# A sequence mixer and FFN kernel: another order of the first loads, later loads in parts, and a new instruction order

## The chip, the cores and the metric

The kernel runs on one core of a Trainium2 chip. The metric is the device time of one execution in microseconds (us), as the median of runs, and lower is better. Profiles come from one execution each; "span" is the time from its first to its last instruction.

## The reference

Input and output are 2048 positions by 640 channels in bfloat16. What is computed:

```python
def A(q, k, v, shift_k, ssm_k, ssm_D):
    k_shift = sum(pad3(k)[t:t + S] * shift_k[:, 3 - t] for t in range(4))   # four taps
    kv = k_shift * v
    y = causal_convolution(kv, ssm_k) + kv * ssm_D      # over S = 2048, in the reference by FFT
    return q * y

def B(x, w_gate, w_up, w_down):                         # 640 -> 1728 -> 640
    return (silu(x @ w_gate) * (x @ w_up)) @ w_down

h   = A_q + A(layernorm(A_q), A_k, A_v, ...)
out = h + B(layernorm(h), ...)
```

The condensed lines above leave out batch, padding and the FFT calls.

## The kernel before, in words

**Blocks.** The 2048 positions are four blocks j = 0 to 3 of 512, and the 640 channels two halves c = 0, 1 of 320. A block sits on 128 partitions with four neighbouring positions each (b = 0 to 3), so that a k tile holds seven rows of 640 per partition: four own ones and three of halo for the taps.

**Per block and half.** kv_block makes kv: four multiplications with taps (kvm), additions (kva) and the product with v (kvv). In blocks 0 and 1 VectorE adds; in blocks 2 and 3 POOL issues accumulating transfers instead (kvd, line 1006), three per half, one after the other. The filter ssm_k is loaded and turned, in blocks 0 and 1 by TensorE (ktr, line 738, then the copies kte), in blocks 2 and 3 by a transposing load. Block 0 is transformed with dense tables den (dfK, dfX; the inverse is di). Blocks 1 to 3 use a two-stage transform: stage one (s1K, s1X), a shuffle between partitions by transfers on SP (shK, shX), stage two (s2K, s2X), products on VectorE (m1, m2, ac, cr, ci, all through line 831), the inverse (i2, shuffles rs, i1). All matmuls but the transposes have line 625, all PSUM evictions line 608 or 611 on ACT, 609 on VectorE.

**LayerNorm and FFN.** The first LayerNorm takes its sums on ACT (lines 960, 967), the second from bn_stats on VectorE (921). Both take the reciprocal root on POOL (nr, line 937: nr0j for the first norm of block j, nr1j for the second), then VectorE's nm (939), the normalized tiles hn (ACT 947 or VectorE 946), their transposes on TensorE (tr, line 1132) and evictions te. The FFN of a block has 13 pairs of five 512-wide matmuls (gu) and a last one for both, silu on ACT (line 1160), the product gm on VectorE, and eight columns of 14 or 15 matmuls for the down projection (dn). The FFN of one block fills TensorE while the next is mixed.

**What sets the order.** Every operation is recorded with its reads and writes. The list _ORDER gives each a rank, _WHO forces some evictions to ACT or VectorE, and a planner (schedule, with durations and a model of transfers, dma_model) deals the operations out in rank order to the engines as their inputs and buffers become free. Each engine then runs its list in that fixed order. Transfers go through the queues of SP, ACT and POOL, each in its order; weight pieces on POOL (wg, wu, gul, wd) wait for the piece before the last, and the first for x of block 1. The tile KIN that takes the k of a block has one buffer, so kin2 waits for block 1's last read of it.

Names of loads: taps (the four tap rows), kraw (a filter half; 256 KB and 64 KB pieces), kin, vin, x (a block of k, v, q), den00 to den13 (eight pieces of 256 KB of the dense tables), tab (the other tables), drow (ssm_D). In block 0 the k rows are the cells "m" and "s" of tile KIN0, "z" its zeroed first rows; all tap multiplications wait for all three.

Of the kernel before, what the change touches and what calls it, by code (L numbers as in the profile page):

```python
# [10 lines left out]
ALU = mybir.AluOpType  # L11
# [5 lines left out]
295 0 2 15 16 249 250 1 3 4 6 5 7 8 9 11 12 13 14 18 17 19 20 21 22 23 25 24 26 27 28 29 30 31 32 254 255 258 259 666 262 263 266 267 270 271 274 275  # L17
278 279 282 286 290 291 294 298 299 287 302 303 283 305 306 641 642 645 646 649 650 653 654 658 661 662 665 657 670 673 337 674 677 678 682 251 685
686 690 692 693 1093 1089 1090 1094 1097 1098 1101 1102 1105 1106 1109 1110 1113 1114 1117 1118 1121 1122 1125 1126 1129 1130 1133 1134 1137 1138 1140
1141 1489 1490 1493 1494 1497 1498 1501 1502 1505 1506 49 1509 1510 1513 1514 1517 1518 1521 1522 1525 1526 1529 1530 1533 1534 238 1537 1538 1540  # L20
1541 310 314 315 319 1176 323 324 328 332 333 341 342 697 701 702 706 710 711 719 720 724 728 729 1145 1149 1150 1154 1158 1159 1163 1167 1168 1172
1177 1545 1549 1550 1554 922 1558 715 1559 1563 1567 1568 1572 1576 1577 236 237 239 240 241 242 243 244 245 246 247 248 34 35 36 33 37 38 39 40 41 10
42 43 44 45 46 48 50 51 52 53 54 55 56 73 892 74 75 76 82 83 84 85 91 92 93 94 100 101 102 103 57 58 59 60 61 62 63 64 65 66 67 68 69 70 71 72 99 77
78 79 80 81 86 87 88 89 90 95 96 97 98 104 105 106 107 108 109 110 111 112 113 114 115 116 117 118 119 120 121 122 123 124 125 126 127 128 129 130 131
132 133 134 1429 151 152 153 154 160 161 162 163 169 170 171 172 178 179 180 181 135 136 137 138 139 140 141 142 143 144 145 146 147 148 149 150 155
156 157 158 159 164 165 166 167 168 173 174 175 176 177 182 183 185 186 187 188 189 190 191 192 193 194 195 196 197 198 199 200 201 202 203 204 205
206 207 184 208 209 1255 210 211 212 213 214 215 216 217 218 219 220 221 222 223 224 225 226 227 228 229 355 356 357 358 359 360 361 362 383 384 385
386 387 388 389 390 391 392 47 393 394 395 396 397 398 230 231 232 399 400 401 402 363 364 365 417 366 367 368 369 370 371 372 373 374 375 376 1561
377 378 379 380 381 382 403 404 405 406 407 431 408 432 409 410 411 412 413 414 415 416 418 419 420 421 422 423 424 425 426 427 428 429 430 435 436
437 438 439 440 441 442 451 443 444 445 446 447 448 449 450 452 453 454 455 456 457 458 459 460 461 462 463 464 433 434 465 466 467 468 469 470 471  # L30
472 473 474 475 476 477 478 479 480 481 482 483 484 485 486 487 488 490 491 492 513 514 515 516 517 518 519 520 521 522 523 524 525 526 527 528 233
234 235 529 530 531 532 493 494 496 497 498 499 500 502 503 504 505 506 507 508 509 533 510 534 511 535 512 536 537 538 539 540 541 542 543 544 545
546 308 547 548 549 551 552 554 555 556 557 558 559 560 561 562 565 550 566 567 568 553 569 570 571 572 573 574 575 576 577 578 579 580 581 582 583
584 771 585 586 587 588 589 590 591 592 593 594 563 564 595 596 597 598 599 600 601 602 603 495 604 605 606 607 608 609 610 611 612 613 614 343 344
345 346 347 348 349 350 351 352 353 354 615 616 617 793 618 620 621 622 623 624 619 625 626 627 628 629 630 632 633 634 635 636 631 637 638 730 731
732 733 734 735 736 737 738 739 740 741 742 755 756 757 758 759 760 761 762 783 784 785 787 788 789 790 791 792 794 795 796 797 798 799 800 801 802
763 764 765 766 767 768 769 770 772 773 779 774 780 775 781 776 782 777 803 778 804 805 806 807 808 809 810 811 812 1346 813 814 815 816 817 818 819
820 821 822 823 824 825 826 827 828 830 831 832 833 834 835 836 839 829 840 841 842 843 844 845 846 847 848 849 850 851 852 853 854 855 856 857 858
859 860 861 862 863 864 865 866 867 868 869 870 871 872 874 873 875 876 877 878 879 880 883 884 885 886 887 888 889 890 837 838 881 882 891 893 894
895 896 897 898 899 900 901 902 903 904 905 906 907 908 909 910 911 912 913 914 915 916 937 938 939 940 941 681 942 943 944 945 946 947 948 949 950  # L40
951 952 953 954 955 956 917 918 919 920 921 923 924 925 926 927 928 929 930 931 932 933 934 935 936 957 958 959 960 961 962 963 964 965 966 967 968
969 970 971 972 973 974 975 976 977 979 980 981 982 983 984 985 986 987 988 989 786 990 993 994 995 996 997 998 999 1000 1001 1002 1003 1004 1005 1006
1007 1008 1010 1011 1012 1147 1013 1014 1015 1016 1009 1017 1018 1019 1020 1021 1022 1023 1024 1025 1026 1027 1028 1029 1030 1031 1032 1033 978 1034
1037 689 1038 1039 1040 1041 1042 1043 1044 991 992 1035 1036 1045 1046 1047 1048 1049 1050 1051 1052 1053 1054 1055 1056 1057 1058 1059 1060 1061
1062 743 744 745 746 747 748 749 750 751 752 753 754 1063 1064 1065 1066 1067 1068 1069 1204 1070 1071 1072 1180 1073 1181 1074 1182 1075 1183 1076
1184 1077 1078 1079 1080 1081 1082 1083 1084 1085 1086 1178 1179 1185 1186 1187 1188 1189 1190 1203 1205 1206 1207 1208 1209 1210 1231 1232 1233 1234
1235 1236 1237 1238 1239 1240 1241 1242 1243 1244 1245 1246 1247 1248 1249 1250 1211 1212 1213 1214 1215 1216 1217 1218 1219 1220 1221 1222 1223 1224
1225 1226 1227 1228 1229 1230 1251 1252 1253 1254 1256 1257 1258 1259 1260 1261 1262 1263 1264 1265 1266 1267 1268 1269 1270 1271 1272 1273 1274 1275
1276 1277 1278 1279 1280 1283 1284 1285 1286 1288 1289 1290 1291 1292 1287 1293 1294 1295 1296 1297 1298 1299 1300 1301 1302 1303 1304 1305 1306 1307
1308 1309 1310 1311 1312 1281 1282 1313 1314 1315 1316 1317 1318 1319 1320 1321 1322 1323 1324 1325 1326 1336 1327 1328 1329 1330 1331 1332 1333 1334  # L50
1335 1337 1338 1339 1340 1361 1362 1363 1364 1366 501 1367 1368 1369 1370 1371 1372 1373 1374 1375 1376 489 1377 1378 1379 1380 1341 1342 1343 1344
1345 1347 1348 1349 1350 1351 1352 1353 1354 1355 1356 1357 1358 1359 1360 1381 1382 1383 1384 1385 1386 1387 1388 1389 1390 1391 1392 1393 1394 1395
1396 1397 1398 1399 669 1401 1402 1403 1404 1405 1406 1407 1408 1409 1410 1413 1414 1415 1416 1417 1418 1419 1420 1421 1422 1423 1365 1424 1425 1426
1427 1428 1440 1431 1432 1433 1434 1435 1436 1437 1438 1430 1439 1441 1444 1442 1411 1412 1443 1445 1446 1447 1448 1449 1450 1451 1452 1453 1454 1455
1456 1457 1458 1459 1460 676 1461 1462 1191 1192 1193 1194 1195 1196 1197 1198 1199 1200 1201 1202 1463 1464 1465 1466 1467 1468 1469 1470 1471 1472
1473 1474 1475 1476 1477 1478 1479 1480 1481 1482 1483 1484 1485 1486 252 253 256 257 260 261 264 265 268 269 272 273 276 277 280 281 284 285 288 289
292 293 296 297 300 301 304 307 309 311 312 313 316 317 318 320 321 322 325 326 327 329 330 331 334 335 336 338 339 340 639 640 643 644 647 648 651
652 655 726 656 659 660 663 664 667 668 671 672 675 679 680 683 684 687 1491 688 691 694 695 696 698 699 700 703 704 705 707 708 709 712 713 714 716
717 718 721 722 723 725 727 1087 1088 1091 1092 1095 1096 1099 1100 1103 1104 1107 1108 1111 1115 1116 1119 1400 1120 1123 1124 1127 1112 1128 1131
1132 1135 1136 1139 1142 1143 1144 1146 1148 1151 1152 1153 1155 1156 1157 1160 1161 1162 1164 1165 1166 1169 1170 1171 1173 1174 1175 1487 1488 1492  # L60
1495 1496 1499 1500 1503 1504 1507 1508 1511 1512 1515 1516 1519 1520 1523 1524 1527 1528 1531 1532 1535 1536 1539 1542 1543 1544 1546 1547 1548 1551
1552 1553 1555 1556 1557 1560 1562 1564 1565 1566 1569 1570 1571 1573 1574 1575
"""
_WHO = (
    "......................................................................................................................................................"
# [38 lines left out]
class Prog:  # L104
# [18 lines left out]
    def op(self, engs, fns, reads=(), writes=(), prio=0, reserve=(), after=(), dma=None, name=""):  # L123
        o = Op()
# [345 lines left out]
def bass_sequential_preLN__ssm_conv_h3__swiglu_ffn__prompt_kernel(  # L470
# [6 lines left out]
    R = 4  # L477
# [836 lines left out]
```

## Time and profile before

| | |
|---|---|
| median of 3 runs | 319.65 us (317.93 to 324.96) |
| the profiled execution | 320.28 us, span 318.5 us |
| busy: TensorE, VectorE, ACT, POOL | 289.2, 236.6, 195.7, 42.1 us |
| bytes moved, mean rate | 41.94 MB, 132 GB/s |
| granted TensorE clock, mean | 0.989 |
| first dense matmul; first gate matmul; first matmul of the last FFN | 17.44; 62.16; 271.12 us |

In timelines a line gives start, duration, engine, source line, operation, output <- input, shapes, count, and in brackets the idle time before it and what ended it. SPq, ACTq and POOL DMA lines are issues of transfers, not the transfers. L-numbers are lines of the kernel before; in the new file the same functions stand 5 to 12 lines further down.

### The profile page before, as it was taken

Reading aid. Unit: us, or ns where it says so; the run is one execution under the profiler, and the core shown is the slowest. Engines: PE = TensorE matmul, PEld = TensorE weight load, DVE = VectorE, ACT = ScalarE, POOL = GpSimd, SP = SyncE. Lnnn points to the kernel's source line nnn. Section 1 sums busy time; section 2 is a strip of 40 time slices with the busy share of each in tenths; the row PEclk is TensorE's granted clock in tenths of the full one; section 3 lists DMA queues with packets and bytes.
Section 4 is the critical chain, followed back from the end, with each engine's and each line's share of the span. In section 5 each row is a group of like instructions: output and inputs, shape, how many; then the busy total and the mean of one; then the engine's idle time right before and its main releaser. Section 6 shows DMA issues by size and latency. Waiting matters only on the chain.

```text
span 318.5 us, 5166 instructions
## 1 busy us (share of the span) xinstructions
PE 289.2 (91%) x1844; PEld 154.9 (49%) x1844; DVE 236.6 (74%) x456; ACT 195.7 (61%) x469; POOL 42.1 (13%) x52
## 2 busy tenths in 40 slices
PE   3399998789959999979999999988999999999996
PEld 0165764334424356645433475543444566444574
DVE  1869999559677999897899999998287847223331
ACT  4269898997955864946874857598985314222200
POOL 0020432530111014100112000421100001000000
PEclk9999999699999999999999999999999999999999
DMA  7999585865673659734914301545310120000011
GB/s 184 348 414 238 167 260 190 293 225 171 142 196 75 176 136 171 221 137 105 284 21 65 126 21 64 145 126 144 84 62 21 43 82 23 21 0 2 0 41 43
DMA packets 29789, 41.94 MB, mean 132 GB/s; under 512 B 7954, under 2 KB 24627, under 8 KB 29253
## 3 DMA queue, kind: packets, MB, share of 16 engines
q1 hardware_dynamic: 23106, 25.43, 24.8%
q0 software_dynamic: 5808, 15.48, 19.6%
q10 hardware_dynamic: 850, 0.69, 0.8%
q8 instruction: 15, 0.25, 0.3%
q14 instruction: 10, 0.08, 0.1%
HBM read 20.63 MB, written 2.62 MB: 73 GB/s over the span
## 4 chain that ended last, share of the span: by engine, by line
PE 55%; DVE 17%; ACT 10%; DMA 10%; SPq 3%; issue 2%; ACTq 1%; POOL 0%; DVEq 0%
PE ps L625 53%; DVE sb L831 15%; DMA sb<-sb 6%; ACT sb L608 5%; DMA sb<-in_A_ssm_k_dram 4%; SPq L616 3%; ACT sb L947 2%; DVE stt L921 1%; ACT sb L611 1%; ACT sb L1160 1%; PE ps L738 1%; ACTq L616 1%; PE ps L1132 1%; ACT sb L967 1%; DVE sb L1091 0%
## 5 line engine op out<-in xcount | busy, mean ns | idle before, releaser
L625 PE MATMUL ps<-sb 128*128 128x320 bf16 (+2 forms) x1204 | 222.9, 339 | 6.7 <-ACT sb L608 3.4
L831 DVE TENSOR_TENSOR sb<-sb 128x1280 bf16<-128x1280 bf16 (+2 forms) x244 | 157.7, 698 | 19.2 <-ACT sb L608 6.9
L625 PEld LDWEIGHTS ps<-sb 128*128 128x128 bf16 (+2 forms) x1204 | 114.6, 98 | 97.0 <-issue 6.8
L608 ACT ACTIVATE sb<-ps 128x320 bf16<-128x320 f32 (+1 forms) x264 | 103.4, 489 | 38.7 <-PE ps L625 26.7
L831 DVE TENSOR_TENSOR sb<-ps,sb 128x512 bf16<-128x512 f32 (+1 forms) x96 | 56.5, 602 | 51.3 <-PE ps L625 50.7
L625 PE MATMUL ps<-sb,tab 128*64 128x320 bf16 (+2 forms) x512 | 66.7, 306 | 11.5 <-DMA sb<-sb 5.5
L1160 ACT ACTIVATE sb<-ps 128x512 bf16<-128x512 f32 (+1 forms) x56 | 33.8, 603 | 42.1 <-PE ps L625 42.0
L625 PEld LDWEIGHTS ps<-sb,tab 128*64 128x64 f16 (+2 forms) x512 | 31.1, 101 | 49.6 <-issue 15.1
L947 ACT ACTIVATE sb<-sb,stt 128x320 bf16<-128x320 bf16 (+1 forms) x35 | 24.3, 727 | 10.7 <-DVE stt L939 10.7
L1006 POOL DMA_DIRECT2D sb<-sb x12 | 12.3, 1023 | 94.9 <-DVE sb L831 77.5
L611 ACT ACTIVATE sb<-ps 128x320 bf16<-128x320 f32 x48 | 17.4, 452 | 8.0 <-PE ps L625 7.9
L937 POOL TENSOR_TENSOR stt<-stt 128x2 f32<-128x2 f32 (+1 forms) x12 | 12.5, 1042 | 67.4 <-DVE stt L936 67.4
L921 DVE BATCH_NORM_STATS2 stt<-sb 128x6 f32<-128x320 bf16 x32 | 13.9, 472 | 0.0
L967 ACT ACTIVATE sb<-sb,stt 128x640 bf16<-128x640 bf16 x16 | 13.4, 839 | 0.6 <-DVE stt L963 0.5
L738 PE MATMUL ps<-sb 128*128 128x128 bf16 (+1 forms) x48 | 7.3, 254 | 6.4 <-DMA sb<-in_A_ssm_k_dram 6.4
L960 ACT ACTIVATE sb<-sb 128x640 bf16<-128x640 bf16 x16 | 11.9, 741 | 0.8 <-DMA sb<-in_A_q_dram 0.7
L738 PEld LDWEIGHTS ps<-sb 128*128 128x128 bf16 (+1 forms) x48 | 4.2, 117 | 10.3 <-DMA sb<-in_A_ssm_k_dram 7.1
L1132 PE MATMUL ps<-sb 128*128 128x128 bf16 x80 | 7.0, 241 | 2.0 <-ACT sb L608 1.9
L1132 PEld LDWEIGHTS ps<-sb 128*128 128x128 bf16 x80 | 5.6, 107 | 3.6 <-DVE sb L831 1.1
L946 DVE TENSOR_SCALAR sb<-sb,stt 128x640 bf16<-128x640 bf16 (+1 forms) x13 | 5.8, 451 | 1.1 <-PE ps L1132 0.8
L936 DVE TENSOR_SCALAR stt<-stt 128x2 f32<-128x2 f32 (+1 forms) x12 | 1.9, 160 | 4.8 <-ACT sb L967 4.8
L616 POOL DMA_DIRECT2D sb<-in_B_w_down_dram x6 | 4.3, 722 | 7.4 <-DMA sb<-in_B_w_down_dram 6.9
(26 smaller groups left out, 37.5 us busy)
## 6 DMA issues: line engine op xcount, KB each, us to landing
sb<-sb SPq DMA_DIRECT2D x72, 160.0 KB, 2.6
sb<-sb POOLq DMA_DIRECT2D x12, 320.0 KB, 4.3
out_dram<-sb SPq DMA_DIRECT2D x16, 160.0 KB, 1.8
sb<-in_A_k_dram POOLq DMA_DIRECT2D x2, 1120.0 KB, 7.9
sb<-cst_den SPq DMA_DIRECT2D x8, 256.0 KB, 11.6
sb<-in_B_w_down_dram POOLq DMA_DIRECT2D x3, 480.0 KB, 5.4
sb<-in_A_v_dram SPq DMA_DIRECT2D x2, 640.0 KB, 12.5
sb<-in_A_q_dram SPq DMA_DIRECT2D x2, 640.0 KB, 12.7
```

Source lines behind the costliest of these rows:

```text
L608: fns = {"act": lambda a: a.activation(out=dst(), in_=src(), func=ACTF.Copy), "dve": lambda v: v.tensor_copy(out=dst(), in_=src())}
L611: fns = {"act": lambda a: a.activation(out=dst(), in_=src(), func=ACTF.Copy, scale=scale), "dve": lambda v: v.tensor_scalar(out=dst(), in0 ...
L616: fns = [(lambda g, d=d, s=s: g.dma_start(d(), s())) for d, s in subs]
L625: return lambda t: t.matmul(o(), l(), r(), start=st, stop=sp)
L738: return t.transpose(B16(pt, b // 2, (b % 2) * CW + d * 128, pr), src, V(IDN, 0, pr, 0, pr))
L831: return lambda v: v.tensor_tensor(out=o(), in0=a(), in1=b_(), op=op)
L921: vec(dve1(CW, False), lambda v: v.bn_stats(st6(l, j, b, c), V(xt, b * D + c * CW, CW)), [(xt, (b, c))], [(ST, ("s", l, j, b, c))], prio, ...
L937: P.op({"pool": 1.05}, lambda g: g.tensor_tensor(out=y, in0=va, in1=stt[:, 420:420 + hi - lo], op=ALU.pow), c1 + [(ST, "half")], c3, prio, ...
L947: "act": lambda a: a.activation(out=dst(), in_=src(), func=ACTF.Identity, scale=rs(l, j, b), bias=tmv(l, j, 3)[:, b:b + 1])},
L967: P.op({"act": act_c(D) + 0.3}, lambda a, b=b, jt=jt: a.activation(out=V(jt, 0, D), in_=V(xt, b * D, D), func=ACTF.Square, bias=tmv(l, j, ...
L1132: fns = [lambda t, k=k, d=d, pk=pk: t.transpose(B16(pk, 0, d * 128, 128), V(hn[k], d * 128, 128), V(IDN, 0, 128)) for d in range(5)]
L1160: P.op({"act": act_c(n)}, lambda a: a.activation(out=dst(), in_=src(), func=ACTF.Silu), rd, wr, -1000, name=f"si{nm}", after=after)
```

## The change

1. *First loads.* Filter half 0 of block 0 (kraw00) goes to the head of SP's queue, then the four own k rows of all 128 partitions in one transfer ("m"), then the three halo rows of partitions 1 to 127 in two ("h"). The first tap multiplication waits for "m" alone. v and filter half 1 follow the first four den pieces, x follows the last but one; drow goes to ACT, which issues no filter or k load any more.
2. *Parts.* The k loads of blocks 2 and 3 are issued as four transfers of 32 partitions, v and x as two of 64, and each accumulating transfer as two of 64 partitions. Blocks 0 and 1 keep whole loads.
3. *The planner.* Other numbers in its model (shuffle issue, shuffle and transpose spacing, half clock at the start and in the filter turns), and new lists _ORDER and _WHO (not shown, 1578 ranks). They change no instruction but its place and, for some evictions, its engine.

The diff from the loads on, without the lists and the planner's clock:

```diff
@@ -658,9 +663,13 @@
         def load_kv(j, prio):
             kt = kins[j] = P.tile(f"kin{j}", "KIN")
             vt = vins[j] = P.tile(f"vin{j}", "VIN")
-            dma([(lambda: V(kt, 0, 7 * D), lambda: dram(K2, (B * j - 3) * D, [[R * D, 128], [1, 7 * D]]))], 1147, [], [(kt, c) for c in range(2)], prio,
+            def rows(t, src, o, n, k):
+                w = 128 // k
+                return [(lambda p=p: V(t, 0, n, p, p + w), lambda p=p: dram(src, o + R * D * p, [[R * D, w], [1, n]])) for p in range(0, 128, w)]
+
+            dma(rows(kt, K2, (B * j - 3) * D, 7 * D, 4 if j > 1 else 1), 1147, [], [(kt, c) for c in range(2)], prio,
                 name=f"kin{j}", eng="pool" if j > 1 else "sp")
-            dma([(lambda: V(vt, 0, 4 * D), lambda: dram(V2d, B * j * D, [[R * D, 128], [1, 4 * D]]))], 655, [], [(vt, c) for c in range(2)], prio + 1,
+            dma(rows(vt, V2d, B * j * D, 4 * D, 2 if j > 1 else 1), 655, [], [(vt, c) for c in range(2)], prio + 1,
                 name=f"vin{j}", eng="pool" if j > 1 else "sp")
 
         def kraw_rows(t, j, c, prio, eng):
@@ -685,7 +694,8 @@
 
         def load_x(j, prio):
             t = xts[j] = P.tile(f"x{j}", "XH")
-            o = dma([(lambda: V(t, 0, 4 * D), lambda: dram(X2, B * j * D, [[R * D, 128], [1, R * D]]))], 655, [],
+            ps_ = ((0, 64), (64, 128)) if j > 1 else ((0, 128),)
+            o = dma([(lambda a=a, b=b: V(t, 0, 4 * D, a, b), lambda a=a, b=b: dram(X2, (B * j + R * a) * D, [[R * D, b - a], [1, R * D]])) for a, b in ps_], 655, [],
                     [(t, (b, c)) for b in range(4) for c in range(2)], prio, name=f"x{j}", eng="pool" if j > 1 else "sp")
             if j == 1:
                 front["x1"] = [o]
@@ -699,16 +709,13 @@
             for c in range(2):
                 kraws[0, c] = P.tile(f"kraw0{c}", "TK")
 
-            def kin(p0, p1, o=0):
-                return (lambda: V(KIN0, o * D, (7 - o) * D, p0, p1), lambda: dram(K2, (R * p0 - 3 + o) * D, [[R * D, p1 - p0], [1, (7 - o) * D]]))
-
-            dma([kin(16, 128), kin(1, 16)], 1140, [], [(KIN0, "m")], -2001, name="kin0")
-            dma([kin(0, 1, 3)], 10, [], [(KIN0, "s")], -2003, eng="act", name="kin0z")
-            kraw_rows(kraws[0, 0], 0, 0, -2000, "act")
-            kraw_rows(kraws[0, 1], 0, 1, -1990, "act")
-            front["v0"] = [dma([(lambda: V(VIN0, 0, 4 * D), lambda: dram(V2d, 0, [[R * D, 128], [1, R * D]]))], 655, [], [(VIN0, c) for c in range(2)], -1990,
-                               name="v0")]
-            dma([(lambda: V(DROW, 0, D, 0, 1), lambda: dram(A_ssm_D, 0, [[D, 1], [1, D]]))], 1, [], [(DROW, 0)], -1980, name="drow")
+            def kin(p0, p1, lo, hi):
+                return (lambda: V(KIN0, lo * D, (hi - lo) * D, p0, p1), lambda: dram(K2, (R * p0 - 3 + lo) * D, [[R * D, p1 - p0], [1, (hi - lo) * D]]))
+
+            kraw_rows(kraws[0, 0], 0, 0, -2010, "sp")
+            dma([kin(0, 128, 3, 7)], 655, [], [(KIN0, "m")], -2001, name="kin0")
+            dma([kin(16, 128, 0, 3), kin(1, 16, 0, 3)], 490, [], [(KIN0, "h")], -2000, name="kin0h")
+            dma([(lambda: V(DROW, 0, D, 0, 1), lambda: dram(A_ssm_D, 0, [[D, 1], [1, D]]))], 1, [], [(DROW, 0)], -1980, eng="act", name="drow")
 
             def den_piece(h, iv, prio):
                 o = (iv * 4 + h) * 1024
@@ -716,9 +723,12 @@
 
             for h in range(R):
                 den_piece(h, 0, -1970 + h)
-            load_x(0, -1960)
+            front["v0"] = [dma([(lambda: V(VIN0, 0, 4 * D), lambda: dram(V2d, 0, [[R * D, 128], [1, R * D]]))], 655, [], [(VIN0, c) for c in range(2)], -1966,
+                               name="v0")]
+            kraw_rows(kraws[0, 1], 0, 1, -1965, "sp")
             for h in range(R):
-                last = den_piece(h, 1, -1950 + h)
+                last = den_piece(h, 1, -1960 + h)
+            load_x(0, -1950)
             front["den"] = [last]
             dma([(lambda: tab[:, :], lambda: tab_dram.ap())], 700, [], [(TAB, 0), (TAB, 1)], -1930, name="tab")
 
@@ -739,6 +749,7 @@
 
                     fns.append(f)
             turned[j, c] = pe(fns, 128, 37, [(kr, 0), (IDN, 0)], tc(pt), prio, reserve=[(kt, 0), (kt, 1)], name=f"ktr{j}{c}")
+            turned[j, c].slow = True
             for k in range(2):
                 evac(lambda k=k: V(kt, k * 2 * CW, 2 * CW), lambda k=k: B16(pt, k, 0, 2 * CW), 2 * CW, [(pt[k], 0)], [(kt, 0)] if k == 0 else [(kt, 1)], prio, fast=True,
                      name=f"kte{j}{c}")
@@ -988,22 +999,22 @@
             t0 = P.tile("t0", "TMP")
             t1 = P.tile("t1", "TMP")
 
-            def v4(t):
-                return V2(t, 0, CW, 4, CW)
-
-            def kw(o):
-                return V2(kt, o * D + c * CW, D, 4, CW)
+            def v4(t, a=None):
+                return V2(t, 0, CW, 4, CW, *((a, a + 64) if a is not None else ()))
+
+            def kw(o, a=None):
+                return V2(kt, o * D + c * CW, D, 4, CW, *((a, a + 64) if a is not None else ()))
 
             def mul(dst, jj):
                 vec(dve2(W4), tt(lambda: v4(dst), lambda: kw(3 - jj), lambda: tapb(jj), ALU.mult),
-                    ([(kt, c)] if j else [(kt, x) for x in "msz"]) + [(TAPS, (jj, c))], [(dst, 0)], prio, name=f"kvm{j}{c}")
+                    ([(kt, c)] if j else [(kt, x) for x in ("mhz" if jj else "m")]) + [(TAPS, (jj, c))], [(dst, 0)], prio, name=f"kvm{j}{c}")
 
             def add():
                 vec(dve2(W4), tt(lambda: V(t0, 0, W4), lambda: V(t0, 0, W4), lambda: V(t1, 0, W4), ALU.add),
                     [(t0, 0), (t1, 0)], [(t0, 0)], prio, name=f"kva{j}{c}")
 
             def acc(src, cells):
-                P.op({"pool": 1.0}, [lambda g: g.dma_start(v4(t0), src(), accum_op=ALU.add)],
+                P.op({"pool": 2.0}, [lambda g, a=a: g.dma_start(v4(t0, a), src(a), accum_op=ALU.add) for a in (0, 64)],
                      [(t0, 0)] + cells, [(t0, 0)], prio, dma=(656, "acc"), name=f"kvd{j}{c}")
 
             mul(t0, 0)
@@ -1015,12 +1026,12 @@
                 mul(t1, 3)
                 add()
             else:
-                acc(lambda: v4(t1), [(t1, 0)])
+                acc(lambda a: v4(t1, a), [(t1, 0)])
                 mul(t1, 2)
                 vec(dve2(W4), tt(lambda: kw(0), lambda: kw(0), lambda: tapb(3), ALU.mult),
                     [(kt, c), (TAPS, (3, c))], [(kt, c)], prio, name=f"kvm{j}{c}")
-                acc(lambda: kw(0), [(kt, c)])
-                acc(lambda: v4(t1), [(t1, 0)])
+                acc(lambda a: kw(0, a), [(kt, c)])
+                acc(lambda a: v4(t1, a), [(t1, 0)])
             hv = lambda: V2(vt, c * CW, D, 4, CW)
             kv_last[j, c] = vec(dve2(W4), tt(hv, hv, lambda: v4(t0), ALU.mult), [(t0, 0), (vt, c)], [(vt, c)], prio, name=f"kvv{j}{c}")
 
@@ -1259,13 +1270,14 @@
             kb, kind = o.dma
             if kind == "shuffle":
                 s = max(issued, dmafree[0])
-                dmafree[0] = s + 0.3
+                dmafree[0] = s + 0.45
                 return s + 1.65 + (1.6 if link[0] > issued else 0.0)
             if kind == "store":
                 return issued + 1.3
             if kind == "turn":
                 s = max(issued, link[0] + 1.0 if link[0] > issued + 2.0 else 0.0, turn[0])
-                turn[0] = s + 4.9
+                turn[0] = s + 3.4
+                dmafree[0] = max(dmafree[0], s + 2.4)
                 return turn[0]
             s = max(issued + (1.3 if o.eng == "pool" else 0.9), link[0])
             link[0] = s + kb / 322.0
```

What it makes of the queues, by name (a star gives the transfers of one operation):

```
SP before:   taps kin0*2 v0 drow den00 den02 den01 den03 x0 den10 den11 den12 den13 tab kin1 vin1 kraw10*2 kraw11*2 x1 ...
SP after:    taps kraw00*2 kin0 kin0h*2 den00 den01 den02 den03 v0 kraw01*2 den10 den11 den12 x0 tab den13 kraw11*2 kin1 vin1 kraw10*2 x1 ...
ACT before:  ident kin0z kraw00*2 kraw01*2 (then work)
ACT after:   ident drow (then work)
POOL before: dadd dadd nr00 wg0 wu0 wg1 wu1 wg2 wu2 gul nr10 nr10 gul wd kin2 wd wd nr01 wd wd wdl kvd20 vin2 kvd20 kvd20 kvd21 ...
POOL after:  dadd dadd nr00 wg0 wu0 wg1 wu1 wg2 wu2 kin2*4 gul gul nr10 nr10 wd wd kvd20*2 wd wd wd wdl vin2*2 nr01 kvd20*2 kvd20*2 ...
```

The heads of the other lists, to block 0's first transposes (TensorE) and second normalized tiles (VectorE), with runs of one kind shortened:

```
TensorE before: ktr00 ktr01 dfK0h0 dfX0 (h0-h3) dfK0 (h1-h3) di0h0 di0h1 dfX1, di0h2, di0h3 dfK1 ktr10 di1 with s1K10, s1X10 ktr11 s2X10 (5 of 8) tr00
TensorE after:  ktr00 dfK0 (h0, h1, half of h2) dfX0 dfK0 (rest) di0h0 di0h1 ktr01 di0h2 di0h3 dfX1 dfK1 ktr10 di1 with s1X10, s1K10 ktr11 s2X10 (8) s2K10 (1) tr00
VectorE before: kvm00 kvm00 kva00 ... kvv00 kvm01 kvm01 kva01 m1000 ... kvv10 ... nm10 kvm11 ... hn01 nm10 kvm11 kva11 hn03 kvv11
VectorE after:  kvm00 kte00 kvm00 kva00 ... kvv00 kvm01 kvm01 kva01 kvm01 m1000 ... kvv10 ... kva11 l1m0 va10 kvv11 nm10 hn01 nm10 kte11 hn03
end, before:    ... dn230 dn231 (10 of 14) tr30 tr30 dn231 (4) tr31 tr31 gu31
end, after:     ... dn230 (10 of 14) tr30 tr30 dn230 (4) tr31 tr31 dn231 (14) gu30
```

## The prediction

> **What bounds the kernel now.** I read the page first (busy shares, the chain), then the timeline of the first 30 us, the stretches of 10 us, the waits of TensorE, and the timeline of single engines where the chain changes hands.
>
> ```profile
> span 318.5 us, 5166 instructions
> PE 289.2 (91%) x1844; PEld 154.9 (49%) x1844; DVE 236.6 (74%) x456; ACT 195.7 (61%) x469; POOL 42.1 (13%) x52
> ...
> PE 55%; DVE 17%; ACT 10%; DMA 10%; SPq 3%; issue 2%; ACTq 1%; POOL 0%; DVEq 0%
> ```
>
> TensorE is the bound, but not in every stage: 45% of the chain is not its own. The losses are in two places. The first is the front:
>
> ```profile
> 9.14 9.64 DVE L831 TENSOR_TENSOR sb<-sb 128x1280 bf16<-128x1280 bf16 x11 [6.56 <-DMA sb<-in_A_k_dram]
> ...
> 12.58 2.09 PE L738 MATMUL ps<-sb 128*128 128x128 bf16 x12 [5.65 <-DMA sb<-in_A_ssm_k_dram]
> ...
> 17.44 8.47 PE L625 MATMUL ps<-sb 128*128 128x320 bf16 x52
> 21.50 4.55 DVE L831 TENSOR_TENSOR sb<-sb 128x640 bf16<-128x640 bf16 x8 [2.72 <-ACT sb L608]
> ```
>
> The dense transforms of block 0 start at 17.44, behind the filter turns. VectorE waits for k until 9.14, again until 21.50, and then hardly at all up to 59.5: its work, not TensorE's, sets when block 0 reaches its second LayerNorm.
>
> ```profile
> 50.00:60.00 10.00, 6.90 (x50) 3.64 (x49) 9.96 (x28) 9.74 (x23) 5.30 (x7) 0.87 0.59 175
> 60.00:70.00 10.00, 8.73 (x49) 3.47 (x48) 3.11 (x6) 9.94 (x24) 4.01 (x5) 0.78 0.76 286
> ```
>
> Columns: stretch, its length, busy PE, PEld, DVE, ACT, POOL, granted clock, DMA share, GB/s. TensorE is idle 4.4 us between 50 and 70, and part of that stretch runs at a lower clock (0.87, 0.78; in stretches of 2 us it is 0.50 from 58 to 64). From 70 on these holes, in TensorE's own timeline, are nearly all that is left, the second place:
>
> ```profile
> 89.95 1.52 PE L625 MATMUL ps<-sb,tab 128*128 128x320 bf16 x10 [1.15 <-DMA sb<-sb]
> 95.62 0.33 PE L625 MATMUL ps<-sb,tab 128*64 128x320 bf16 x2 [2.40 <-DMA sb<-sb]
> 140.75 1.10 PE L625 MATMUL ps<-sb,tab 128*128 128x320 bf16 x6 [1.88 <-ACT sb L608]
> 215.98 1.02 PE L625 MATMUL ps<-sb,tab 128*64 128x320 bf16 x8 [0.92 <-DMA sb<-sb]
> 271.12 44.52 PE L625 MATMUL ps<-sb 128*128 128x512 bf16 x247 [1.11 <-ACT sb L608]
> ```
>
> **The change, part by part.** The profiled execution took 320.28 us (span 318.5, 1.8 around it), 0.6 above the median 319.65. The sum is made against 320.28.
>
> *The ring's order.* Before, SP issues k (980 KB, then 15 rows) first and ACT the filter; 980 KB land 5.9 us after issue at 1.16, at 7.1, and the 15-row piece with the halo lets VectorE go only at 9.14. After, SP issues filter 00 (320 KB) and the 128 k rows (640 KB): 960 KB, so again about 7.1 for the first multiply, which now needs these alone. The halo is 488 KB more; at the 216 and 373 GB/s of the first two stretches that is 1.3 to 2.3 us, so 8.4 to 9.4; I take 8.5. Filter 00 should land near 4.5 to 5; its turn (2.09 us) ends near 7, and its copy, now second on VectorE (0.48), fits before the halo. ACT no longer issues six load pieces, so it starts its tap evictions (from 5.71) some 2.7 us earlier.
>
> VectorE then: seven operations of 0.83 from 8.5 end kv of column half 0 at 14.3 (15.9 before). Four operations of half 1 follow to 17.6. The first X transform of h0 is eight matmuls after 14.3, at most 2.1 us at half rate, and two evictions of 0.45: 17.3. So the 2.72 us wait shrinks to nothing, and the products start at 17.6, not 21.5, with one multiply and one copy more behind them (1.3): a lead of 5.2 us. TensorE keeps up: its 20 K matmuls stand before X and run from about 9, when the first dense table has landed (1.7 MB by then). The second filter half and v come later in the ring, at some 13 and 14 us, but its turn stands behind the first inverse transforms, past 20.
>
> *What the lead is worth.* From the products to the second hn tile of block 0 the new VectorE order has the three filter copies in place of two K evictions and one copy (no difference), one normalization less (0.37) and the last kv multiply of block 1 ahead (0.82): 4.75 us left. That multiply and two more stand ahead of the first normalization too, so ACT's hn00 and the first LayerNorm transpose (57.42) come 2.9 us sooner; but TensorE has four spectrum groups more behind it (0.7): 3.6 us. What is late next is POOL: rstd of block 0 (54.32) now stands behind four kin2 issues and both gul pieces, which wait for the up and gate weights.
>
> ```profile
> 46.06 0.87 POOL L616 DMA_DIRECT2D sb<-in_B_w_up_dram  x1 [1.61 <-DMA sb<-in_B_w_up_dram]
> 54.32 2.21 POOL L937 TENSOR_TENSOR stt<-stt 128x2 f32<-128x2 f32 x2 [2.81 <-DVE stt L936]
> ```
>
> The last weight piece landed 6.4 us after 46.06; the weight chain starts behind block 0's first rstd (32.1 before; the new VectorE order has 12.1 us of work from the products to it, so 29.7), 2.4 us sooner, so it ends at about 50.1; a gul issue of 0.87 puts the rstd at 51.0, where VectorE needs it (50.9). So it holds, by nothing to spare. Bounds for the front: 5.2 if nothing gives it back; -1.5 if kin2's 1120 KB, which now cross the first shuffles of block 1 instead of following them, delay these as other bulk transfers do.
>
> *Half clock.* TensorE was 4.9 us busy in the 6 us at half clock, of which 2.5 would be saved. The nine spectrum pairs and unbroken transposes ahead of the first FFN may keep it full or not: 0 to 2.5, I take 0.5, since it still waits there.
>
> *Bulk in parts.* kin 2 and 3 go in four, v, x and the twelve accumulates in two: 22 more POOL issues of 0.55 to 1.0 us, 12 to 22 us, which lie under POOL's waits (77 us on VectorE alone). What can be had shows in the chain, in order of time:
>
> ```profile
> 91.03 4.54 DMA sb<-sb
> 135.52 4.64 DMA sb<-sb
> 211.04 5.45 DMA sb<-sb
> ```
>
> In the list of DMA issues (count, KB each, us to landing) the medians are shorter:
>
> ```profile
> sb<-sb SPq DMA_DIRECT2D x72, 160.0 KB, 2.6
> sb<-sb POOLq DMA_DIRECT2D x12, 320.0 KB, 4.3
> ```
>
> A shuffle takes 2.6 us, but 4.5 to 5.5 where POOL has an accumulate or a bulk load out (issued at 90.3, 128.6, 210.2); four of the holes above, 6.35 us, are of this kind. Parts that come 0.6 to 1 us apart leave room between, but the bytes are the same. Bounds: all 6.35, or a loss of 2 when a shuffle meets two issues instead of one; a third, 2.1.
>
> [...]
>
> *The order's end.* The 1.11 us hole at 271.12 waits for the eviction of the last transposes; the new order puts 14 matmuls (1.9 us at 0.136) behind them instead of FFN 3's first. Gain 1.0 (0 to 1.1).
>
> Sum: 3.6 + 0.5 + 2.1 + 1.0 = 7.2; 320.28 - 7.2 = 313.1 us.
>
> **The rivals.** *No change within 2%:* the front's lead is given back between 50 and 70, where ACT is busy 9.7 and 9.9 of 10 us and POOL's rstd has no slack. For it: those rows. Against it: ACT does the K evictions before 17 now, when it idled. Front 0.7 for the spectrum groups, 1.0 at the end, 0.7 from the parts: 317.9 us. This is also what an order that only moves waits would give.
>
> *Slower:* the halved accumulates. The three of a kv block are serial, each waiting for the landing of the last; a second issue of about 1 us each makes a chain 3 us longer, in four chains, and VectorE stops in order at the multiply that needs them. Once this shows already (225.32, 3.1 us). If all four are exposed 12 us are added, with the front's 3.6 and the 1.0 kept and no gain from parts: 320.28 + 12 - 4.6 = 327.7. It decides only if more than three chains are exposed and TensorE runs out of FFN matmuls; against it, three of four kv multiplies came with no wait at all, and FFN work fills the holes.
>
> **How the numbers follow.** Forecast 0.56, no change 0.26, slower 0.18. A measurement of this kernel can tell about 2%, 6.4 us, from no change. The forecast's own range is 308 to 317; its bounds (front 5.2, clock 2.5, parts 6.35, end 1.1) could reach 305.1, which is all of them together. Range 306.5 to 320.5, which takes in the no-change case and leaves out most of the slower one. The forecast lies just past the 2% line at 313.3, so part of its chance (0.08) falls to no change and part of the second case's (0.06) could go to faster: 0.54, 0.28, 0.18.
>
> **What would show it.** Right: first multiply near 7, products near 17.6, first LayerNorm transpose near 54, shuffles at about 3 us in the DMA list, holes near 90, 95 and 140 halved, none before the last FFN. Wrong: rstd of block 0 still at 54, a first transpose at 57, shuffles of block 1 above 4 us beside kin2, or VectorE waits above 2 us on accumulates.

## The result and the profile after

The changed kernel took 323.39 us as the median of 44 runs, the kernel before 323.14 us beside it; the ratio is 1.0076 (95% interval 1.005 to 1.0102). By this ratio the change costs 0.8%, where a gain of 2.2% was forecast. Runs of one kernel spread by 2 to 3%, and the ratio compares for each kernel only the faster ones, within 1.5% of its fastest; over all runs the medians differ by 0.1%, so that the small loss depends on this choice, but the missing gain does not. The time lies above the range (320.5), also if the ratio is put on the 320.28 us of the forecast (322.7). The profiled execution took 321.65 us.

From here on, a percentage is a difference of such ratios to the kernel before, run beside each other, and 1% is 3.2 us.

From the page of the kernel after, first the span, the busy times and the chain:

```profile
span 319.8 us, 5188 instructions
PE 293.2 (92%) x1844; PEld 158.9 (50%) x1844; DVE 235.5 (74%) x451; ACT 199.0 (62%) x474; POOL 58.7 (18%) x74
...
PE 71%; ACT 12%; DMA 7%; DVE 6%; issue 2%; POOL 1%; SPq 1%; ACTq 0%; DVEq 0%
```

TensorE's share of the chain rose from 55 to 71%, which looks like success, but it is also busy 4 us longer for the same 1844 matmuls: part of its work ran at a lower clock (0.961 granted in the mean, 0.989 before). POOL is busy 16.6 us longer. The front did what it was meant to; VectorE's first multiply, then TensorE's timeline:

```profile
7.21 0.83 DVE L842 TENSOR_TENSOR sb<-sb 128x1280 bf16<-128x1280 bf16 x1 [4.63 <-DMA sb<-in_A_k_dram]
```

```profile
10.05 10.18 PE L630 MATMUL ps<-sb 128*128 128x320 bf16 x55 [3.18 <-DMA sb<-cst_den]
...
54.28 0.46 PE L630 MATMUL ps<-sb,tab 128*64 128x320 bf16 x4 [1.34 <-DMA sb<-sb]
59.79 2.59 PE L630 MATMUL ps<-sb,tab 128*64 128x320 bf16 x14 [5.05 <-DMA sb<-sb]
62.62 0.71 PE L1143 MATMUL ps<-sb 128*128 128x128 bf16 x5 [0.24 <-ACT sb L958]
...
154.02 1.25 PE L630 MATMUL ps<-sb,tab 128*128 128x320 bf16 x8 [3.52 <-DMA sb<-sb]
```

The dense transforms start at 10.05 instead of 17.44. Then TensorE waits 6.4 us for block 1's first shuffles, and the first LayerNorm transpose comes at 62.62 instead of 57.42: a lead of 7 us has become a delay of 5. A second hole, 3.52 us at 154, was 0.66 before. The holes at 90, 95, 140 and 271 are gone; between 208 and 216 the holes add up to 3.2 us, 2.2 before. In the chain in order of time the holes have one name, a transfer from SBUF to SBUF:

```profile
50.22 9.53 DMA sb<-sb
...
146.09 7.69 DMA sb<-sb
```

In stretches of 10 us (columns as in the prediction) the first hole is paid for by its idle time, and a lower clock follows it:

```profile
50.00:60.00 10.00, 3.60 (x29) 2.09 (x29) 6.09 (x22) 4.65 (x13) 5.50 (x8) 0.81 0.92 202
60.00:70.00 10.00, 9.31 (x53) 4.23 (x49) 4.48 (x7) 9.67 (x20) 4.89 (x6) 0.51 0.78 191
```

From 60 to 70 TensorE is busy 9.31 us at a granted clock of 0.51 (0.78 before). What was beside the shuffles, from POOL's timeline and the list of DMA issues:

```profile
49.60 2.02 POOL L621 DMA_DIRECT2D sb<-in_A_k_dram  x4 [4.38 <-DVE sb L1102]
```

```profile
sb<-sb SPq DMA_DIRECT2D x72, 160.0 KB, 2.2
sb<-sb POOLq DMA_DIRECT2D x24, 160.0 KB, 4.8
sb<-in_A_k_dram POOLq DMA_DIRECT2D x8, 280.0 KB, 5.9
```

kin2 in four parts is issued at 49.60, while the X shuffles of block 1 go out on SP (49.55 to 55.08). And the parts gain little or nothing in landing: half an accumulate takes 4.8 us, where the whole took 4.3, and a quarter of k 5.9, where the whole took 7.9.

### The profile page after: what moved, and what is told of

Read it like the earlier page. It is cut to its first block, busy times and chain, and to the rows that moved or that the text cites. A ratio compares the mean times of both kernels' runs of the same rounds, so it can differ in the third digit from the quotient of the medians.

```text
span 319.8 us, 5188 instructions
## 1 busy us (share of the span) xinstructions
PE 293.2 (92%) x1844; PEld 158.9 (50%) x1844; DVE 235.5 (74%) x451; ACT 199.0 (62%) x474; POOL 58.7 (18%) x74
## 4 chain that ended last, share of the span: by engine, by line
PE 71%; ACT 12%; DMA 7%; DVE 6%; issue 2%; POOL 1%; SPq 1%; ACTq 0%; DVEq 0%
PE ps L630 70%; ACT sb L613 5%; DMA sb<-sb 5%; DVE sb L842 5%; ACT sb L958 3%; DMA sb<-cst_den 2%; ACT sb L971 2%; PE ps L1143 1%; POOL stt L948 1%; SPq L621 1%; ACT sb L616 1%; ACT sb L1171 0%; ACT sb L978 0%; DVE sb L957 0%; DVE sb L614 0%
## 5 line engine op out<-in xcount | busy, mean ns | idle before, releaser
L630 PE MATMUL ps<-sb 128*128 128x320 bf16 (+2 forms) x1204 | 227.3, 344 | 8.8 <-DMA sb<-cst_den 3.2
L630 PEld LDWEIGHTS ps<-sb 128*128 128x128 bf16 (+2 forms) x1204 | 116.4, 100 | 102.0 <-issue 12.9
L842 DVE TENSOR_TENSOR sb<-ps,sb 128x512 bf16<-128x512 f32 (+2 forms) x96 | 56.6, 603 | 53.6 <-PE ps L630 52.0
L630 PE MATMUL ps<-sb,tab 128*128 128x320 bf16 (+2 forms) x512 | 67.0, 317 | 12.0 <-DMA sb<-sb 9.9
L630 PEld LDWEIGHTS ps<-sb,tab 128*128 128x128 f16 (+2 forms) x512 | 32.8, 103 | 47.9 <-issue 17.8
L1017 POOL DMA_DIRECT2D sb<-sb x24 | 21.9, 1079 | 79.4 <-DVE sb L842 69.3
L958 ACT ACTIVATE sb<-sb,stt 128x320 bf16<-128x320 bf16 (+1 forms) x38 | 25.8, 729 | 13.5 <-DVE stt L950 13.5
L948 POOL TENSOR_TENSOR stt<-stt 128x2 f32<-128x2 f32 (+1 forms) x12 | 14.1, 1176 | 54.5 <-DVE stt L947 54.4
L957 DVE TENSOR_SCALAR sb<-sb,stt 128x640 bf16<-128x640 bf16 (+1 forms) x10 | 4.1, 414 | 8.3 <-ACT sb L958 7.3
L760 POOL TENSOR_TENSOR sb<-sb 1x320 bf16<-1x320 bf16 x2 | 2.2, 1102 | 25.2 <-DVE sb L614 18.4
```

The costliest lines, as they stand in the source:

```text
L630: return lambda t: t.matmul(o(), l(), r(), start=st, stop=sp)
L842: return lambda v: v.tensor_tensor(out=o(), in0=a(), in1=b_(), op=op)
L948: P.op({"pool": 1.05}, lambda g: g.tensor_tensor(out=y, in0=va, in1=stt[:, 420:420 + hi - lo], op=ALU.pow), c1 + [(ST, "half")], c3, prio, ...
L958: "act": lambda a: a.activation(out=dst(), in_=src(), func=ACTF.Identity, scale=rs(l, j, b), bias=tmv(l, j, 3)[:, b:b + 1])},
L1017: P.op({"pool": 2.0}, [lambda g, a=a: g.dma_start(v4(t0, a), src(a), accum_op=ALU.add) for a in (0, 64)], [(t0, 0)] + cells, [(t0, 0)], pr ...
```

## The experiments

Two theories. *Place*: the loss comes from where the new order puts bulk, above all kin2 beside the first shuffles. *Parts*: it comes from the cutting itself. In all variants below the planned costs were held, so that every engine's order is that of the kernel named, but for what the text says is moved.

| variant | ratio to before | interval |
|---|---|---|
| after | 1.0076 | 1.005 to 1.0102 |
| e1: after, kin2 late | 0.986 | 0.9798 to 0.9922 |
| e2: after, kin2 whole | 0.9914 | 0.9864 to 0.9965 |
| e3: after, all whole | 0.9797 | 0.9722 to 0.9872 |
| e4: before, all cuts | 1.0401 | 1.0323 to 1.048 |
| e5: e3, kin2 late | 0.9764 | 0.969 to 0.9838 |
| e6: after, accumulates whole | 1.0048 | 0.9999 to 1.0097 |
| e7: after, cut along the row | 0.9839 | 0.9736 to 0.9943 |
| e8: e3 with the old first loads | 1.002 | 0.9968 to 1.0072 |
| e9: e7, kin2 late | 0.9713 | 0.9673 to 0.9753 |
| e10: e9, two more moves | 0.9787 | 0.9746 to 0.9828 |
| e11: before, accumulates cut | 1.0141 | 1.0096 to 1.0186 |
| e12: before, cut along the row | 0.9928 | 0.9893 to 0.9964 |
| e13: after, every 2nd or 4th partition | 0.9827 | 0.9733 to 0.9922 |
| e14: before, new first loads | 1.000 | 0.994 to 1.006 |

### Place or parts: e1 to e4

**e1**, after scheduling:

```diff
+        behind("kin2", "nr10", 2)      # on POOL: behind the second nr10
```

> The kernel after, with one thing moved: the four kin2 issues stand on POOL behind both rstd of block 0 (nr10) instead of ahead of gul, so they come after the shuffles of X in block 1; all other engine orders are those of the kernel after. Theory 'place' (the loss comes from bulk issued beside shuffles that TensorE waits for): the 5.05 us wait at s2X10h1 shrinks below 1, the shuffles land in 2 to 3 us, hn00 comes at 56 to 57, the half clock from 56 on lasts 7 us or less, and the time falls by 6 to 9 us, to 313 to 316. Theory 'parts' (the loss comes from the cutting: small pieces over few partitions are slow wherever they stand): the slow pieces now meet the K shuffles and what follows, and the time falls by 0 to 3 us, to 319 to 322.

Measured: 0.986, 2.2% less than after, the 7 us of "place". The 5.05 us wait is 0.28.

**e2** and **e3**: kin2 alone, then all loads and accumulates whole.

```diff
-dma(rows(kt, K2, (B * j - 3) * D, 7 * D, 4 if j > 1 else 1), ...
+dma(rows(kt, K2, (B * j - 3) * D, 7 * D, 1), ...
...
-P.op({"pool": 2.0}, [lambda g, a=a: g.dma_start(v4(t0, a), src(a), accum_op=ALU.add) for a in (0, 64)],
+P.op({"pool": 2.0}, [lambda g: g.dma_start(v4(t0), src(None), accum_op=ALU.add)],
```

> The kernel after, with kin2 in one transfer of 128 partitions at the same place (its planned cost kept, so that every engine's order is that of the kernel after). Theory 'place': 1.1 MB cross the shuffles as before, the wait at s2X10h1 stays 4 to 6 us and the time within 2 us of 321.7. Theory 'parts': one transfer of 128 partitions ends sooner, the wait is 2 us or less and the time 316 to 318.

> The kernel after with every cut undone (kin, vin, x and the twelve accumulating transfers whole, planned costs kept, so the engines' orders are unchanged): the new front and the new order alone. Theory 'place': the holes at s2X10h1 and at i1200 stay, 320 to 323. Theory 'parts': both shrink by half or more, 315 to 317. If the cuts help in the middle as the prediction took it (2.1 us), it is slower than the kernel after, 323 to 325.

Measured: 0.9914 and 0.9797. kin2 whole recovers 1.6%, all whole 2.8% (9 us; with the two intervals 6.5 to 11.5), although kin2 still crosses the shuffles. TensorE's timeline of e3:

```profile
57.60 3.34 PE L630 MATMUL ps<-sb,tab 128*64 128x320 bf16 x18 [3.56 <-DMA sb<-sb]
...
149.92 1.25 PE L630 MATMUL ps<-sb,tab 128*128 128x320 bf16 x8 [0.71 <-ACT sb L613]
```

One wait of 3.56 us is left of the 6.4, and the hole of 3.52 has become 0.71.

**e4**: the kernel before with the diff's cuts.

> The kernel before with only the cuts added (kin 2 and 3 in four, vin, x and accumulates in two), in the engine orders of the kernel before. Theory 'place': the extra issues lie under POOL's waits and the holes near 90, 95 and 140 keep their size: within 1.5 us of before. Theory 'parts': 2 to 4 us slower than before. The prediction's term: 2.1 us faster (bounds -6.35 to +2), the holes at 89.95 and 95.62 shrinking.

Measured: 1.0401. In the old order, where kin2 stands behind the shuffles, the same cuts cost 4%, 13 us. In its TensorE timeline two of the holes that were to shrink, and one more, have grown (1.15, 1.88 and 0.66 before):

```profile
92.30 2.83 PE L625 MATMUL ps<-sb,tab 128*128 128x320 bf16 x10 [3.66 <-DMA sb<-sb]
...
146.67 1.10 PE L625 MATMUL ps<-sb,tab 128*128 128x320 bf16 x6 [2.72 <-ACT sb L608]
161.70 0.98 PE L625 MATMUL ps<-sb,tab 128*128 128x320 bf16 x6 [2.54 <-DMA sb<-sb]
```

So the cutting is the loss. "Place" comes on top: a late kin2 is worth 2.2% beside these parts (e1); e5 tries what it is worth without them.

### Both undone, and the accumulates alone: e5, e6, e11

**e5** is e3 with e1's line.

> All cuts undone (as in e3_all_whole) and kin2 behind both rstd of block 0 (as in e1_kin2_late). If the two costs add (cuts 9 us by e3, place of kin2 about 3.5 us idle plus 3.4 us of half clock that e3 still has near 57), 308 to 311, 3 to 4% under before. Rival: what kin2 frees early it costs later, since the first products of block 1 stand on VectorE behind the first multiplies of block 2, which wait for kin2 (4.97 us in e1): 313 to 315, no better than e3.

Measured: 0.9764, 0.3% less than e3 and not to be told from it. The two gains do not add. With whole transfers the place of kin2 costs little: when it is late, VectorE waits 2.9 us for kin2 where TensorE had waited for the shuffles.

**e6** has of e3's edits only the accumulates' (the last two lines of that diff).

> The kernel after with only the twelve accumulating transfers whole; kin, vin and x stay in parts. Theory 'serial chain' (the halves of an accumulate land no sooner than the whole, 4.8 against 4.4 us, and each of the three waits for both): about half of e3's gain, 3 to 5 us, 317 to 320; the hole at i1200 shrinks. Rival, the cut loads beside shuffles are all of it: 1 us or less, 322 to 323.

Measured: 1.0048, 0.3% less than after, again not to be told from it. In the new order no cost of the accumulates' halves can be told. Of the cut loads kin2 alone is 1.6% (e2); kin3, vin and x were not tried apart.

**e11** is the kernel before with the change's cut of the accumulates alone:

```diff
-P.op({"pool": 1.0}, [lambda g: g.dma_start(v4(t0), src(), accum_op=ALU.add)],
+P.op({"pool": 1.0}, [lambda g, a=a: g.dma_start(v4(t0, a), src(a), accum_op=ALU.add) for a in (0, 64)],
```

> The kernel before with only the twelve accumulates cut into two of 64 partitions (loads whole). The slower rival's mechanism (three serial transfers per half block, each about 1 us longer, four chains) would give up to 12 us, so 328 to 332, most of the 4% of e4. By e6, where making them whole gained nothing that could be told, it is the cut loads that cost: 319 to 322 beside 319.7.

Measured: 1.0141. In the old order the halved accumulates cost 4.5 us, about a third of e4's 13 and less than half of the slower rival's 12. Its mechanism, VectorE stopped by the longer chains, shows only faintly: VectorE waits 4.1 us for accumulates, in four places, against 3.1 in one before. TensorE's holes at 91.46 and 221.06, which end with a transfer from SBUF to SBUF, grew more (3.02 and 2.71 us; 1.15 and 0.92 before).

### Issues, few partitions, or neighbours: e7, e12, e13

**e7** keeps the number of transfers, but cuts along each partition's row:

```diff
-return V2(t, 0, CW, 4, CW, *((a, a + 64) if a is not None else ()))
+return V2(t, 0, CW, 4, CW) if a is None else V2(t, a * CW, CW, 2, CW)     # a in (0, 2)
...
+def cols(t, src, o, cuts):      # kin by (0, 2, 4, 6, 7), vin and x by (0, 2, 4)
+    return [(lambda a=a, b=b: V(t, a * D, (b - a) * D), lambda a=a, b=b: dram(src, o + a * D, [[R * D, 128], [1, (b - a) * D]])) for a, b in zip(cuts, cuts[1:])]
```

> The kernel after with the same number of transfers, but cut along the row: every part goes over all 128 partitions with a half or a quarter of each partition's bytes (kin by 2, 2, 2 and 1 rows, vin, x and the accumulates by 2 and 2). Theory 'issues' (the cost is that there are more transfers, each with its issue and its fixed time): as slow as the kernel after, 321 to 324. Theory 'few partitions' (32 or 64 rows use the engines badly): most of e3's gain comes back, 315 to 317.

Measured: 0.9839, within the error of e3. So it is not the number of issues. Its list of DMA issues, where a half now does land sooner than the whole of before (4.3):

```profile
sb<-sb POOLq DMA_DIRECT2D x24, 160.0 KB, 3.6
sb<-in_A_k_dram POOLq DMA_DIRECT2D x6, 320.0 KB, 4.5
```

**e12** is the same cut in the kernel before.

> The kernel before with all cuts of the change, but along the row (128 partitions each), in the orders of the kernel before. If only the few partitions were bad and parts as such let shuffles through (the prediction's term, 2.1 us): 317 to 318.5. If parts do nothing: 319.5 to 321. If issues cost as well: 322 to 325.

Measured: 0.9928, 2.3 us faster, the size of the prediction's term. Its profiled execution, 321.76 us, is one of the slowest of its ten and does not show the gain as a whole. In it the hole at 140.75 is gone, 153.91 is little changed (0.87), 95.62 is as it was, and 89.95 grew:

```profile
93.02 1.52 PE L625 MATMUL ps<-sb,tab 128*128 128x320 bf16 x10 [1.56 <-DMA sb<-sb]
98.67 0.33 PE L625 MATMUL ps<-sb,tab 128*64 128x320 bf16 x2 [2.39 <-DMA sb<-sb]
```

**e13** has the diff's parts, 32 or 64 partitions each and packets of the same size, but a part takes every fourth or second partition:

```diff
-    return [(lambda p=p: V(t, 0, n, p, p + w), lambda p=p: dram(src, o + R * D * p, [[R * D, w], [1, n]])) for p in range(0, 128, w)]
+    return [(lambda p=p: dst(p), lambda p=p: dram(src, o + R * D * p, [[R * D * k, 128 // k], [1, n]])) for p in range(k)]
+    # dst(p): partitions p, p + k, p + 2k, ... ; vin, x and the accumulates with k = 2
```

> The kernel after with the same number of transfers, each over the same number of partitions (32 or 64) and with packets of the same size, but a part takes every fourth or every second partition instead of neighbours. [...] Theory 'few rows' (32 or 64 packets spread badly over the engines wherever they go): as the kernel after, 320 to 324, halves at 4.7 or more.

Measured: 0.9827, 315.83 us, where "few rows" has 320 to 324. In its list of DMA issues:

```profile
sb<-sb POOLq DMA_DIRECT2D x24, 160.0 KB, 3.6
sb<-in_A_k_dram POOLq DMA_DIRECT2D x8, 280.0 KB, 4.5
```

The same bytes, packets and issues land in 3.6 and 4.5 us instead of 4.8 and 5.9. In TensorE's timeline of e13 the second hole has shrunk to 0.89 us, but at the first shuffles 3.79 us of one wait are left, and 0.48 of the other:

```profile
58.35 2.60 PE L630 MATMUL ps<-sb,tab 128*64 128x320 bf16 x14 [3.79 <-DMA sb<-sb]
...
149.25 1.25 PE L630 MATMUL ps<-sb,tab 128*128 128x320 bf16 x8 [0.89 <-ACT sb L613]
```

So of the 6.9 us between the spans of the two profiles (319.8 and 312.9) only 1.5 are won by the first LayerNorm transpose (61.17 against 62.62), and 4.8 by the end of the second hole. The packet records of the traces say directly what changed. Median time of one packet on POOL's queue, in ns:

| | before | after | e3 | e13 |
|---|---|---|---|---|
| 8960 bytes (k rows) | 338 | 654 | 338 | 338 |
| 2560 bytes (two of every three accumulates) | 225 | 378 | 222 | 225 |

Only where a part is 32 neighbouring partitions (k) or 64 (accumulates) does a packet take 1.9 or 1.7 times as long. That is the cause of the loss, shown by changing nothing but which partitions a part takes.

### What the first loads are worth: e8, e14

**e8** is e3 with the first loads in the order of before (k whole first, filters on ACT's queue), **e14** the kernel before with the new ones; only these lists and the loads' own pieces differ:

```diff
 # e8
+ring("sp", ["taps", "kin0", "v0", "drow", "den00", "den02", "den01", "den03", "x0", "den10", "den11", "den12", "den13", "tab"])
+ring("act", ["kin0h", "kraw00", "kraw01"])
 # e14
+ring("sp", ["taps", "kraw00", "kin0", "kin0z", "den00", "den01", "den02", "den03", "v0", "kraw01", "den10", "den11", "den12", "x0", "tab", "den13"])
+ring("act", ["drow"])
```

In e8 kin0h stands for the 5 KB of before, in e14 kin0z for the halo.

> All cuts undone (as in e3), but the first loads in the order of the kernel before (k whole first, filters on ACT, v after k, x after the first four den pieces) under the engine orders of the kernel after. Prediction's term for the new ring: 3.6 us plus some clock, so 318 to 319 against 314.4 of e3, first multiply at 9 instead of 7. Rival, the lead is given back at kin2's shuffles and the rest is the order's: 314 to 315.5, not to be told from e3.

Measured: 1.002, so the ring is worth 2.2% (7 us; with the two intervals 4 to 10) in the new order. From e8's VectorE timeline:

```profile
9.49 0.83 DVE L842 TENSOR_TENSOR sb<-sb 128x1280 bf16<-128x1280 bf16 x1 [6.91 <-DMA sb<-in_A_k_dram]
14.96 0.49 DVE L614 COPY sb<-ps 128x640 bf16<-128x640 bf16 x1 [4.65 <-PE ps L748]
```

More is lost than the 1.4 us of the first multiply (8.05 in e3): the copy kte00, second in the new VectorE order, waits for a filter turn that starts at 12.83, and all multiplies stand behind it.

> The kernel before with the new order of first loads alone; every engine keeps the order of the kernel before. If the ring is worth its time by itself (first multiply 2 us sooner): 2 to 3.6 us faster, 316 to 317.7. Rival, it needs the new TensorE order: there the filter turns stand ahead of the dense transforms, and the second filter half, now behind four den pieces, lands near 13, so the first dense matmul stays at 16 to 17.5 and the time within 1 us of before; slower by up to 2 if filter half 1 comes later than before.

Measured: 1.000. In the old TensorE order both filter turns stand ahead of the dense transforms; in the trace the second turn waits for its filter half until 15.13, and the first dense matmul starts at 17.15. So for ring and order alone no gain can be told (1.000 and 1.002; of the ring alone all ten runs have a median of 324.59 us, beside 321.77), and together they are worth 2.0% (0.9797).

Where the two meet shows in TensorE's busy time by stage, in us (granted clock in brackets where it is not 1.00):

| | 0 to 30 | 30 to 75 | 75 to 150 |
|---|---|---|---|
| before | 18.6 | 40.3 (0.92) | 69.2 |
| e8: new order, old loads | 17.5 | 36.1 (0.85) | 73.3 |
| e3: new order, new loads | 23.1 | 36.3 (0.85) | 73.0 |
| after | 24.0 | 34.7 (0.81) | 74.5 |

The new order loses 4 us between 30 and 75 and wins 4 from 75 to 150; the new loads win 5.6 us in the first 30, but only under the new order (18.7 us in e14, 18.6 before).

### The fastest version: e9, and a step too far: e10

**e9** is e7 with e1's line, **e10** is e9 with two lines more:

```diff
+        shift("act", "deX1h2", "q000", True)     # ahead of q000
+        shift("dve", "kvm20", "cr100")           # behind cr100
```

> Cuts along the row (as in e7_cut_by_columns) and kin2 behind both rstd of block 0 (as in e1). e7 stood at 0.984 with 3.7 us of waits at the first shuffles, 0.8 of which e5 kept with kin2 late: 309.5 to 311.5, 0.965 to 0.972 of before. Rival: kin2 late costs again what it frees (e5 waited 2.9 us for it on VectorE), 312 to 314.

Measured: 0.9713, 312.17 against 321.76 us, and 3.6% less than the kernel after: the lowest ratio of all, though the interval of e5 reaches below it, and faster than both kernels. Here the late kin2 gains 1.3% (e7 stood at 0.9839).

> As e9, and two places in engine orders changed: on ACT the two evictions deX1h2 stand ahead of q000 (the hole of 2.74 us at 35 in every variant of the new order waits for them, behind q000 to q003 which wait for rstd), and on VectorE the first two multiplies of block 2 stand behind cr100 instead of ahead of block 1's first products. If both waits lie on the path: 2 us less than e9. If VectorE, busy without a gap from 20 to 55, sets the end of this stage, the hole at 35 goes and nothing is gained by it: within 1 us of e9.

Measured: 0.9787, 0.7% slower than e9. TensorE's timeline of e10:

```profile
35.77 6.18 PE L630 MATMUL ps<-sb 128*128 128x320 bf16 x32 [2.47 <-DVE sb L1101]
...
75.77 0.46 PE L630 MATMUL ps<-sb,tab 128*64 128x320 bf16 x4 [0.94 <-DMA sb<-sb]
```

The hole at 35 kept 2.47 of 2.75 us: with ACT's evictions ahead it waits for VectorE's multiply L1101 instead. And TensorE has six holes of 0.3 to 0.9 us between 75 and 103, 3.7 us in all, where e9 has one of 0.60. Which of the two moves opened them was not tried.

## Why the prediction was wrong

**The step that failed is "bulk in parts".** It was put at a gain of 2.1, with a loss of 2 as its worst. Measured: a loss of 9 us in the new order and 13 in the old one. Its reasoning, that parts leave room for shuffles between them, may hold for parts as such: cut along the row they bring 2.3 us in the old order (e12). In the new order no gain of theirs can be told (e7 against e3, e9 against e5). What it lacked was a look at which partitions a part covers. The bound of 2 counted issues; none of the rows that it used prices a transfer over few partitions, so the bound had to be wider.

**What tells slow parts from fast ones.** It is which partitions they take. A packet of a k part takes 654 ns over 32 neighbouring partitions and 338 when the same count is spread (e13); a half accumulate lands in 4.8 us over 64 neighbours and in 3.6 over every second partition. Either way the accumulate is in two disjoint halves of the same bytes, so the halving is not what makes it slow. Why neighbours are slow, no run here shows.

**kin2 across the first shuffles** had the right place and sign ("shuffles of block 1 above 4 us beside kin2" was named as the sign of failure), but a price of about 5 us (the front's 3.6 down to -1.5). In the profile after it is 6.4 us of waits and a stretch at clock 0.51. Slow parts are not all of it: with kin2 whole, 3.56 us of the waits stay (e3), and 4.27 with parts of every fourth partition, whose packets are as fast as in the whole (e13). But moving it late gains only 0.3% when it is whole (e5), and 1.3% in parts along the row (e9).

**The front was right in its first steps, and so was the order's end.** First multiply 7.21 (7.1 predicted), first dense matmul 10.05 (from about 9), no hole ahead of the last FFN. Without the parts the prediction's terms are 3.6 + 0.5 + 1.0 = 5.1 us; e3 measured 2.0%, 6.5 us (4 to 9). But the sum fits partly by luck. The lead was to bring the first LayerNorm transpose from 57.42 to near 54; it comes at 61.18 in e3, and at 56.70 in e5, where kin2 is out of the way. By 75 us TensorE is 0.4 us ahead in e3, and the gain is made after that, from 75 to 150 (table above): the holes at 90, 95 and 140, of which the parts were to save 2.1 us, are gone in e3 by the new order alone, but for one of 0.65. Nor was it foreseen that ring and order need each other.

**"The rstd holds, by nothing to spare"** failed: it starts at 53.51, not 51.0, 0.8 us before that of the kernel before instead of 3.3. The issues ahead of it on POOL end at 53.40, but they are not what makes it late. Its input comes from VectorE (L947), in after from 53.10 to 53.41, and in e5, where POOL is free in time, the rstd waits 1.73 us for the same input:

```profile
53.10 0.31 DVE L947 TENSOR_SCALAR stt<-stt 128x2 f32<-128x2 f32 x1
```

```profile
53.29 2.24 POOL L948 TENSOR_TENSOR stt<-stt 128x2 f32<-128x2 f32 x2 [1.73 <-DVE stt L947]
```

So VectorE had kept less than 1 us of its lead here; what used up the rest was not taken apart.

**Half clock** had the wrong sign: not 0.5 gained, but a longer stretch. The mean granted clock from 50 to 70 was 0.66 in after, with 6.4 us of waits at the first shuffles, 0.74 in e3 with 3.6 and 0.83 in e1 with 0.6 (0.83 before). It goes with the waits in these; that they cause it was not tried.

**The rivals.** "No change within 2%" is what came about, though not below the time of before (317.9 us was its figure). Its mechanism, a lead given back by 70, is in the trace (by 75 the kernel after is 0.2 us behind in TensorE's busy time), but through the waits for shuffles rather than ACT or the rstd, and the loss by the parts that it did not have outweighs what the order wins later. "Halved accumulates" was real in the old order at 4.5 us (e11) and too small to tell in the new one (e6).

## What to carry to other kernels

When a transfer is cut so that others can pass, try the cut along the row, or let each part take every n-th partition; here parts of neighbouring partitions cost 9 us more than they freed (13 in the old order), and the list of DMA issues shows it at once (a half that lands no sooner than the whole, here 4.8 us against 4.3). A new order of loads and a new order of engines may show nothing each and a gain together (here 1.000 and 1.002, and 0.9797): test them in all four combinations before one is dropped. A change of several parts is best judged part by part: here a gain of 2% and a loss of 2.8% hid in a result that looks like nothing.

## What the hardware showed that was not expected

- In the median, a packet of a part of 32 neighbouring partitions took 1.9 times (654 against 338 ns, k), one of 64 1.7 times (378 against 225 ns, accumulates) as long as in a transfer over all 128; spread over every fourth or second partition it took the same time as in the whole (338 and 225 ns, e13).
- Shuffles of 160 KB, 2.2 us in the median, took 6.9 us (e3) to 9.5 us (after) in the chain beside a bulk load of 1120 KB, whole or cut.
- Half an accumulate costs POOL as much to issue as a whole one (1079 ns in after, 1018 in e3); with the other parts, POOL's busy time rose from 45.3 us (e3) to 58.7 us (after) for the same bytes.
